# Reordering the first matrix products around the transposes at the start of a 2:4 sparse linear layer

## The chip, the cores and the metric

The kernel runs on one core of one Trainium2 chip. The metric is device time in microseconds (us) of one execution; lower is better. Before the change the median was 234.31 us over three executions (234.19 to 234.88).

Names: PE is TensorE, ACT is ScalarE, DVE is VectorE, SP is the engine that issues most loads, POOL is GpSimd. "Lnnn" in a profile is a line of the kernel's source.

## The reference, cut to what matters

```python
B, S, D = 16, 512, 1024
def reference(x, w, b):
    wg = w.reshape(G, M, D)                      # M = 4 rows of w to a group
    mag = jnp.abs(wg)
    order = jnp.argsort(mag, 1)
    thr = jnp.take_along_axis(mag, order[:, M - N:M - N + 1, :], 1)   # N = 2
    mask = (mag >= thr).astype(w.dtype)          # keeps the 2 largest of each 4
    wp = (wg * mask).reshape(D, D)
    return jnp.einsum("bsd,df->bsf", x, wp) + b
```

All types are bf16. The product has 8192 rows (64 tiles of 128), 1024 inputs and 1024 outputs.

## The kernel before

DVE has to prune the weights before the products can begin, so the kernel starts on what is ready first. Tiles 0 to 7 ("packed" tiles) are loaded plainly and transposed on PE; DVE prunes the weights in six pieces, and the products of these tiles with the first half of the inputs take the first four pieces (0 to 3) as DVE finishes them. The other 56 tiles come later through transposing loads. Each engine's program order in this start is a list of tokens:

- `T7a`: four PE transposes of x tile 7 into one of two PSUM banks. `C7a`: ACT copies that bank to SBUF.
- `M7.0x`: two products of tile 7 with the first half (x) of weight piece 0; `y` is the other half; `M7.2` is four products with piece 2.
- `S0b0`: ACT copies a finished PSUM bank of tile pair 0 (tiles 5 and 6) to a staging tile.
- `A0h1`: four products of the next group of tiles. `W1.0q`: two loads that spread pruned weights.

```python
    psum_t = ctx.enter_context(tc.tile_pool(name="psum_t", bufs=2, space=bass.MemoryType.PSUM))
    psum_o = ctx.enter_context(tc.tile_pool(name="psum_o", bufs=6, space=bass.MemoryType.PSUM))
    # ... loads, in program order on SP after the first weight loads:
    load_x(5, 7)
    load_x(0, 2)
    load_w(0, 256, 512)
    load_x(4, 5)
    load_x(2, 4)                 # x for tiles 2 and 3
    load_w(0, 512, 1024)
    # ...
    def transpose(t):            # T
        # ... bank from psum_t (two of them)
        for m in range(4):
            pe(nc.tensor.transpose(tp[:, m, :], xg[:, m, :], ident[:]))
    def copy_xt(t):              # C
        # ...
        act(nc.scalar.copy(xt[:].bitcast(fp32), xpk[t].bitcast(fp32)))
    def mm_piece(t, i, ms):      # M
        # ...
        for m in range(ms.start, ms.stop):
            # ...
            pe(nc.tensor.matmul(ps[:, c0 + d:c1 + d], lhsT=xpk[t][:, m, :], rhs=wp[:, g, m, c0:c1], ...))
    pairs = [(5, 6), (0, 1), (2, 3), (4, 7)]
    # ...
        "pe": (
            "F8 T7a T5a T6a T1a M5.0x M7.0x T0a M6.0x M6.0y M1.0x M7.0y M5.0y T3a M0.0y T4a M1.0y "
            "M0.0x T2a M3.0y M4.0x M3.0x M4.0y M2.0y M2.0x M4.1x M5.1x M0.1x ... "
            "... M3.3 M1.3 A0h0 A2h0 M7.3 A2h1 A1h0 A3h1 A0h1 A3h0 A1h1"
        ),
        "act": (
            "C7a C5a C6a C1a C0a C3a C4a S0b0 C2a S3b0 S1b0 S2b0 ... S1b3 S2b3 W1.0q S3b3 S0b3"
        ),
```

`T6a` waits for `C7a`, because there are two transpose banks; every later T waits in the same way for the C two transposes back.

Of the kernel before, what the change touches and what calls it, by code (L numbers as in the profile page):

```python
# [10 lines left out]
def kernel(  # L11
# [241 lines left out]
    def stage(q, n):  # L253
        if (q, n // 2) not in staged:
# [3 lines left out]

    order = {
        "pe": (  # L260
            "F8 T7a T5a T6a T1a M5.0x M7.0x T0a M6.0x M6.0y M1.0x M7.0y M5.0y T3a M0.0y T4a M1.0y "
            "M0.0x T2a M3.0y M4.0x M3.0x M4.0y M2.0y M2.0x M4.1x M5.1x M0.1x M7.1y M6.1y M2.1y "
            "M1.1y M3.1y M6.1x M4.1y M1.1x M3.1x M0.1y M7.1x M2.1x M5.1y M0.2 M3.2 M7.2 M1.2 M2.2 "
            "M4.2 M6.2 M0.3 M2.3 M5.3 M4.3 M5.2 M6.3 M3.3 M1.3 A0h0 A2h0 M7.3 A2h1 A1h0 A3h1 A0h1 "
            "A3h0 A1h1"
        ),
        "dve": (
            "abs0a hi0a abs0b lo0a hi0b lo0b t20 t10 thr0 mask0x mult0x mask0y mult0y abs1 lo1 hi1 "
# [2 lines left out]
            "thr5 mask5 mult5"  # L271
        ),
        "act": (
            "C7a C5a C6a C1a C0a C3a C4a S0b0 C2a S3b0 S1b0 S2b0 abs3 S3b1 S1b1 S0b1 S2b1 S2b2 S1b2 "
            "S3b2 S0b2 S1b3 S2b3 W1.0q S3b3 S0b3"
        ),
        "sp": (
# [213 lines left out]
```

## Time and profile before

| | before |
|---|---|
| median time | 234.31 us |
| span of the profiled execution | 232.5 us |
| PE busy | 227.5 us (98%) |
| granted clock | 1.00 |
| products after the packed start (L240) | 87% of the chain that ends last |

PE is the bound almost from start to end. The only room for a change of order is the time that PE stands still, and in the first 12 us that is well under 1 us. "Chain" is the sequence of work that ended last, followed backwards from the last instruction.

### The profile page before, as it was taken

To read this page: it belongs to the slowest core of one execution; us is meant where nothing else is said; L and a number is where in the kernel's file an instruction comes from. 1 tells how busy PE (TensorE), PEld (TensorE's weight loads), DVE (VectorE), ACT (ScalarE), POOL (GpSimd) and SP (SyncE) were. 2 spreads that over 40 slices of the span, in tenths; PEclk is the share of its full clock that TensorE was granted. 3 is DMA by queue.
4 is the path that set the end of the run, shared out by engine and by line. 5 is a ranking of instruction groups with operands and counts; after the bars stand their busy time and mean duration, and the time that the engine had idled before them with its cause. 6 is when DMAs were issued, how large, how long until landed. Compare 5 with 4: busy or idle time off the path is not lost.

```text
span 232.5 us, 2829 instructions
## 1 busy us (share of the span) xinstructions
PE 227.5 (98%) x1139; PEld 113.3 (49%) x1158; DVE 108.2 (47%) x185; ACT 13.7 (6%) x27; POOL 17.6 (8%) x15
## 2 busy tenths in 40 slices
PE   8999999999999999999999999999999999999995
PEld 5888444554444444444444444444444444444443
DVE  4999868864244244234334334324424424423434
ACT  2575100000000000000000000000000000000000
POOL 1000199700000000000000000000000000000000
PEclk9999999999999999999999999999999999999999
DMA  6999999996589521992249821696228931122122
GB/s 194 314 249 207 225 177 224 219 327 209 193 187 238 161 76 62 232 263 94 90 85 245 256 93 45 160 256 174 91 90 194 265 128 71 67 90 81 59 89 90
DMA packets 78268, 38.19 MB, mean 164 GB/s; under 512 B 63664, under 2 KB 70576, under 8 KB 78256
## 3 DMA queue, kind: packets, MB, share of 16 engines
q1 hardware_dynamic: 67600, 20.88, 44.0%
q10 hardware_dynamic: 10656, 17.14, 21.1%
q8 instruction: 9, 0.15, 0.3%
q14 instruction: 3, 0.02, 0.0%
HBM read 3.41 MB, written 16.78 MB: 87 GB/s over the span
## 4 chain that ended last, share of the span: by engine, by line
PE 94%; DMA 2%; SPq 1%; issue 1%; DVE 0%
PE ps L240 87%; PE ps L217 5%; DMA x<-in_x_dram 2%; PE tp L240 1%; SPq L100 1%; PE tp L191 0%; DVE o L400 0%
## 5 line engine op out<-in xcount | busy, mean ns | idle before, releaser
L240 PE MATMUL ps<-wp_nat,xb 128*128 128x512 bf16 (+2 forms) x832 | 178.9, 375 | 0.8
L240 PEld LDWEIGHTS <-xb 128*128 128x128 bf16 x848 | 82.4, 98 | 97.6
L400 DVE TENSOR_TENSOR o<-ps,bias_sb 128x512 bf16<-128x512 f32 (+1 forms) x112 | 71.5, 677 | 114.7 <-PE ps L240 110.3
L396 POOL TENSOR_TENSOR st<-st,bias_sb 128x1024 f32<-128x1024 f32 x8 | 16.7, 2127 | 0.0
L217 PE MATMUL ps<-wp,xt 128*128 128x256 bf16 x128 | 15.0, 273 | 0.0
L240 PE MATMUL ps<-wp_nat,xlow 128*128 128x512 bf16 x62 | 14.0, 379 | 0.1
L217 PEld LDWEIGHTS <-xt 128*128 128x128 bf16 x128 | 12.3, 98 | 1.6
L402 DVE TENSOR_TENSOR o<-ps,st 128x512 bf16<-128x512 f32 x16 | 11.1, 691 | 2.8 <-PE ps L240 2.1
L240 PE MATMUL ps<-wp_nat,xlead 128*128 128x512 bf16 x47 | 11.1, 379 | 0.1
L240 PEld LDWEIGHTS <-xlow 128*128 128x128 bf16 x64 | 7.2, 112 | 6.7
L240 PEld LDWEIGHTS <-xlead 128*128 128x128 bf16 x64 | 6.3, 98 | 7.1
L257 ACT COPY st<-ps 128x512 f32<-128x512 f32 x16 | 8.5, 594 | 6.1 <-PE ps L217 4.2
L156 DVE TENSOR_TENSOR wp<-w_sb,mag 128x512 bf16<-128x512 bf16 (+2 forms) x8 | 5.4, 690 | 0.2
L156 DVE TENSOR_TENSOR mag<-mag,hi 128x512 bf16<-128x512 bf16 (+2 forms) x8 | 5.4, 690 | 0.2
L135 PE MATMUL ps<-zeros 128*128 128x128 bf16 (+1 forms) x22 | 4.4, 400 | 1.0 <-DVE zeros L86 1.0
L240 PE MATMUL tp<-wp_nat,xlead 128*128 128x512 bf16 x16 | 4.1, 379 | 0.0
L191 PE MATMUL tp<-ident,x 128*128 128x128 bf16 x32 | 3.6, 260 | 0.3 <-DMA x<-in_x_dram 0.3
L135 PEld LDWEIGHTS <-zeros 128*128 128x128 bf16 x22 | 2.5, 147 | 2.6 <-issue 1.7
L166 DVE TENSOR_SCALAR mag<-w_sb 128x512 uint16<-128x512 uint16 (+2 forms) x6 | 2.7, 469 | 2.3 <-DMA w_sb<-in_w_dram 2.1
L191 PEld LDWEIGHTS <-x 128*128 128x128 bf16 x32 | 3.0, 130 | 0.8 <-DMA x<-in_x_dram 0.6
L156 DVE TENSOR_TENSOR hi<-mag 128x512 bf16<-128x512 bf16 (+2 forms) x7 | 3.2, 460 | 0.3 <-ACT mag L159 0.2
L196 ACT COPY xt<-tp 128x256 f32<-128x256 f32 x8 | 3.0, 375 | 4.3 <-PE tp L191 4.2
(16 smaller groups left out, 14.3 us busy)
## 6 DMA issues: line engine op xcount, KB each, us to landing
out_dram<-o ACTq DMA_DIRECT2D x59, 256.0 KB, 2.5
wp_nat<-wp SPq DMA_DIRECT2D x14, 128.0 KB, 3.4
w_sb<-in_w_dram SPq DMA_DIRECT2D x3, 512.0 KB, 7.0
out_dram<-o ACTq DMA_DIRECT2D x8, 128.0 KB, 1.7
x<-in_x_dram SPq DMA_DIRECT2D x3, 256.0 KB, 4.0
w_sb<-in_w_dram SPq DMA_DIRECT2D x1, 256.0 KB, 4.5
bias_sb<-in_b_dram SPq DMA_DIRECT2D x1, 256.0 KB, 7.0
wp_nat<-wp ACTq DMA_DIRECT2D x2, 128.0 KB, 3.5
```

The costliest lines, as they stand in the source:

```text
L100: return seq(eng, q.dma_start(out_, in_))
L135: pe(nc.tensor.matmul(warm_ps[:, :rep * P], lhsT=zeros[:], rhs=zeros[:, None, :].to_broadcast([P, rep, P]), start=True, stop=True))
L156: dve(nc.vector.tensor_tensor(out, a, b_, op=op))
L166: dve(nc.vector.tensor_single_scalar(self.mag[:, ms, :].bitcast(u16), self.w[:, ms, :].bitcast(u16), 0x7FFF, op=Alu.bitwise_and))
L191: pe(nc.tensor.transpose(tp[:, m, :], xg[:, m, :], ident[:]))
L196: act(nc.scalar.copy(xt[:].bitcast(fp32), xpk[t].bitcast(fp32)))
L217: pe(nc.tensor.matmul(ps[:, c0 + d:c1 + d], lhsT=xpk[t][:, m, :], rhs=wp[:, g, m, c0:c1], start=(new and m == ms.start), stop=(left[(q, n) ...
L240: pe(nc.tensor.matmul(ps, lhsT=xt[:, kt - koff, :], rhs=wp_nat[:, kt, c0:c1], start=(kt == first), stop=(kt == last)))
L257: act(nc.scalar.copy(st[:, n % 2, :, :].rearrange("p t c -> p (t c)"), ps_open.pop((q, n))[:]))
L396: pool(nc.gpsimd.tensor_tensor(st[:], st[:], bias[:, :, None, :].to_broadcast([P, 2, 2, CW]), op=Alu.add))
L400: dve(nc.vector.tensor_tensor(o[:, c0:c1], ps, bias_sb[:, c0:c1], op=Alu.add))
L402: dve(nc.vector.tensor_tensor(o[:, c0:c1].rearrange("p (n c) -> p n c", n=2), ps.rearrange("p (n c) -> p n c", n=2), add, op=Alu.add))
```

## The change

Its intent: keep PE from standing before the transpose of tile 3, whose x arrives late. The first products of tiles 7, 5 and 6 go ahead of the transposes of tiles 1 and 0; the transposes of tiles 3 and 2 go behind more of the first-piece products; ACT's copies follow the new order. Nothing is added or removed.

```diff
         "pe": (
-            "F8 T7a T5a T6a T1a M5.0x M7.0x T0a M6.0x M6.0y M1.0x M7.0y M5.0y T3a M0.0y T4a M1.0y "
-            "M0.0x T2a M3.0y M4.0x M3.0x M4.0y M2.0y M2.0x M4.1x M5.1x ...
+            "F8 T7a T5a T6a M7.0x M5.0x M6.0x T1a T0a M7.0y M5.0y M6.0y M1.0x M1.0y M0.0x T4a M0.0y "
+            "T3a T2a M4.0x M4.0y M3.0x M3.0y M2.0x M2.0y M4.1x M5.1x ...
         "act": (
-            "C7a C5a C6a C1a C0a C3a C4a S0b0 C2a S3b0 ...
+            "C7a C5a C6a C1a C0a C4a S0b0 C3a C2a S3b0 ...
```

## The prediction

> **What bounds the kernel now.** I read the page first, then the chain in order of time, then the waits of PE, then the first 30 us instruction by instruction. The page:
>
> ```profile
> PE 227.5 (98%) x1139; PEld 113.3 (49%) x1158; DVE 108.2 (47%) x185; ACT 13.7 (6%) x27; POOL 17.6 (8%) x15
> ...
> PE   8999999999999999999999999999999999999995
> ...
> PEclk9999999999999999999999999999999999999999
> ...
> PE 94%; DMA 2%; SPq 1%; issue 1%; DVE 0%
> ```
>
> TensorE (PE) is busy in every slice at the full granted clock, and 94% of the chain that ends last is PE. The change reorders PE and ScalarE (ACT) in the first 12 us only, so the question is how much PE stands still there. The chain in order of time says where it starts:
>
> ```profile
> 4.00 5.25 DMA x<-in_x_dram
> 9.25 0.05 issue
> 9.30 0.41 PE tp L191 x4
> 9.71 0.22 PE ps L217 x2
> 9.93 0.22 PE tp L191 x4
> 10.15 0.44 PE ps L217 x4
> 10.59 0.22 PE tp L191 x4
> 10.81 11.35 PE ps L217 x104
> ```
>
> The chain follows PE back without a break only to 9.30 us, and there to the load of x for tiles 2 and 3, issued at 4.00 and landed at 9.25. From 10.81 on it is 104 first-weight-half products back to back. The waits of PE agree; the first is the start of the fillers:
>
> ```profile
> PE ps L135 <- DVE zeros L86: 1.0, 1, 1.0
> PE tp L191 <- DMA x<-in_x_dram: 0.3, 1, 0.3
> ```
>
> The 0.3 understates it, as a matmul's reported end includes its modelled drain. Start to start: the last product before it (M5.0y) starts at 8.725, its slot is 0.109 us, so PE is free at 8.834 and T3 begins at 9.296: 0.46 us lost. The stretches show it (PE busy is the first figure after the comma; the four here are transposes and first products, more products, the wait, and the rest up to M4.1x):
>
> ```profile
> 5.23:7.08 1.85, 1.81 (x18) 1.65 (x17) 1.68 (x5) 0.88 (x3) 0.00 (x0) 1.00 1.06 310
> 7.08:8.84 1.76, 1.76 (x21) 1.51 (x18) 1.62 (x6) 0.95 (x3) 0.00 (x0) 1.00 0.87 282
> 8.84:9.30 0.46, 0.16 (x3) 0.01 (x1) 0.43 (x2) 0.00 (x0) 0.00 (x0) 1.00 0.86 274
> 9.30:11.96 2.66, 2.66 (x30) 2.47 (x31) 2.52 (x8) 1.75 (x5) 0.00 (x0) 1.00 1.05 352
> ```
>
> The other loss is a 0.24 us hole ahead of T6 (last T5 at 5.975 plus 0.107; first T6 at 6.325), which waits until C7 has emptied one of the two transpose banks.
>
> **What the Trainium skill says.** "TensorE: Matmul & The Clock Gate", section "Back-to-back issue gap", gives columns/1.2 ns cold and columns/2.4 + 2.5 ns warm. The trace agrees: transposes (128 columns) start every 0.107 us up to about 7.02 us and every 0.056 after it, products (256 columns) every 0.109. The same page, section "What's actually happening", calls the window that releases the clock free-running, so the 7.02 may move between executions; one trace can't show that. "Perfetto Trace Analysis", section "Tensor Engine Instruction (MATMUL, LD_WEIGHTS)", says a matmul's reported end is an estimate; hence I count start to start. "ScalarE: Activation LUTs", section "What ACT_TABLE_LOAD costs", says back-to-back activations overlap by about 93 ns; here, after a 0.372 us copy (C4 at 10.190), the next starts 0.268 later, an overlap of 0.104.
>
> **The change part by part.** Nothing is added or removed: PE has the same 2318 rows and ACT the same instructions. DVE keeps its order. So the sum is only of waits. I use these handover times from the trace: last transpose start + 0.219 (its duration, warm) + 0.037 to the copy's start; copy 0.372 + 0.05 to the PE instruction that needs it; 0.268 from one copy to the next on a busy ACT, 0.478 after a 0.59 us staging copy. Checked on the old order, this arithmetic puts M4.1x (first product of the second weight piece, where the two orders meet again) at 11.952; the trace has 11.960.
>
> *Part 1, M7.0x M5.0x M6.0x ahead of T1 T0.* To T6's end at 6.75 nothing differs. M7.0x needs C7 (done 6.27) and the first masked weights (6.226): no wait. It runs mostly cold and ends at 7.10; M5.0x ends at 7.32. M6.0x needs C6, done at about 7.37, and its handover at 7.42: a new wait of 0.10. M6.0x, then T1 7.64 to 7.87, T0 to 8.09. The old order had only T1 in the cold stretch; the new has M7.0x there, the same time. T1's and T0's banks have been emptied. So part 1 costs 0.10.
>
> *Part 2, more first products before the late transposes.* From 8.09: M7.0y M5.0y M6.0y M1.0x M1.0y M0.0x, six of 0.218 (C1 and C0 are done at 8.45 and 8.72, before they are needed), then T4 at 9.40 (its x landed at 7.45) and M0.0y at 9.62. T3 comes at 9.84, by which time its x has been there since 9.25: the 0.46 wait is gone, with 0.55 in hand. But T3 and T2 now stand side by side, and T2 takes the bank of T4: T4's last transpose starts at 9.565, C4 runs 9.82 to 10.20, T2 begins at 10.25 where PE was free at 10.06: a new wait of 0.19.
>
> *Part 3, ACT now C4 S0b0 C3 C2.* S0b0 (the staging copy of pair 0) starts 0.268 after C4, at 10.09. C3 must follow it by 0.478, at 10.57, although T3 was ready near 10.3. M4.0x M4.0y fill PE from 10.47 to 10.91; M3.0x needs C3 and starts near 11.00: a new wait of 0.09. C2 follows at 10.84 and holds up nothing. Then four products of 0.218, and M4.1x at 11.87.
>
> *Sum.* Removed 0.46 (0.44 in my arithmetic); added 0.10 + 0.19 + 0.09 = 0.38; rounding and the cold stretch leave a gain of about 0.08 us (11.952 to 11.868).
>
> *Does it reach the end?* PE then has to find later waits no closer than this. The tightest I found: A2h1 at 24.166 needs its four weight blocks, of which the last, landed at 23.51, is used at 24.814: 1.3 us in hand. A0h1 at 26.756 needs S0b3's bank, released at 26.32: about 0.4 in hand. A1h0 at 25.030 has its bank since 23.286. So a gain of 0.1 passes through the whole of the PE stream to the end: 234.31 - 0.08, about 234.2.
>
> **The rivals.**
>
> *The load wait is the whole story.* If the three new waits are absent (other handovers than I took), the gain is 0.46, giving 233.85. For it: the 0.46 is the only PE wait that the profile names after the fillers. Against it: T2 really does need C4, and the two are one M and one T apart.
>
> *The load lands later in most executions.* The old time moves one for one with that landing, the new one has 0.55 of slack. A load 0.3 later in the timed runs than in the profiled one makes the gain 0.38, giving about 233.9. One 0.6 earlier removes the old wait and makes the change lose about 0.38: 234.7. Landing took 5.25 us here, while the median of such loads is 4.0, so both are possible. DMA was 86% busy in that stretch, which speaks for the late side.
>
> *The clock opens at another time.* By the same arithmetic, were it warm from 6.0 the gain would be 0.33, since the old order just waits longer for its load; were it still cold until 8.0, the new order would be 0.28 behind, for it has no wait left to absorb slow matmuls. Against a large move: the timed runs spread over only 0.69 us (234.19 to 234.88).
>
> *Lost later.* ACT is nearer to the bound in 10 to 12 us, and a staging copy that comes later than a bank is needed would halt PE. S3b0 ends near 11.7 and M0.1x, which takes the bank that S3b0 frees in the new order, comes at about 12.3: not bound. This would make it 234.3.
>
> **Range and chances.** Centre 234.2. The gain lies between about -0.4 (an early load or a late clock) and +0.6 (a late load or an early clock); the medians of runs add some 0.3 of their own. That gives 233.6 to 234.8. A gain or a loss of 2% is 4.7 us. The PE idle time in all the first 12 us that this could touch is 0.7 us, and nothing in the diff alters the 220 us that follow, so 2% either way is out of reach except through a disturbed run: 0.01 faster, 0.985 within 2%, 0.005 slower.
>
> **What would show each step.** In the changed profile: the wait of a transpose for the load of x gone from PE's waits; T3 near 9.84; a gap of about 0.1 us before M6.0x at 7.4 and of about 0.2 before T2 at 10.25, released by ACT; C3 starting about 0.48 after S0b0, with M3.0x near 11.0; M4.1x at 11.87; from there the same spacing to the end, with the last product about 0.1 earlier. Part 2 is wrong if PE does not wait before T2; part 3 if C3 is not held by S0b0. The prediction as a whole would be wrong if PE shows new waits after 12 us, if the clock opens later than 7.0, or if the span shrinks by much more than 0.5 us.

## The result, and the profile after

The changed kernel takes 234.20 us (median of four, 234.01 to 234.62) beside 234.25 for the kernel before (median of four). The ratio is 0.9995 with a 95% interval of 0.9972 to 1.0018: the same. Ratios here are the mean time of one kernel's fast runs over the mean of the other's from the same rounds, so they are not quite the ratio of the quoted medians. A plain mean of all runs can differ a little (for no_waits_again, with one execution of 235.75, it gives 1.0001 beside 0.9992).

The page's PE line and its chain by engine have hardly moved:

```profile
PE 227.5 (98%) x1139; PEld 112.8 (49%) x1158; DVE 108.1 (47%) x185; ACT 13.3 (6%) x27; POOL 17.6 (8%) x15
...
PE 96%; DMA 2%; issue 1%; ACTq 0%; ACT 0%; DVE 0%
```

The chain after, in order of time (start, length, what), now reaches back through PE past 9.3 us:

```profile
5.52 0.63 PE tp L191 x4
6.17 0.38 ACT xt L196
6.60 0.38 PE tp L191 x4
6.98 0.44 PE ps L217 x4
7.44 0.39 PE ps L217 x2
7.84 0.45 PE tp L191 x8
8.28 1.31 PE ps L217 x12
9.59 0.22 PE tp L191 x4
9.82 0.22 PE ps L217 x2
10.04 0.22 PE tp L191 x4
10.28 0.38 PE tp L191 x4
10.66 11.47 PE ps L217 x104
```

The load of x for tiles 2 and 3 has left the chain. The waits of PE now name ACT's copies (engine, what waited, for whom: us in total, times, longest):

```profile
PEld L217 <- ACT xt L196: 0.5, 2, 0.3
...
PE tp L191 <- ACT xt L196: 0.2, 1, 0.2
```

PEld is the weight load ahead of a product. Its two waits are those of M6.0x (for C6) and M3.0x (for C3). The 0.2 of the second line is not new: it is T6 waiting for C7, ahead of all that the change touches. From start to start that hole was 0.24 us before and is 0.40 here, where the clock opened earlier and the transposes before T6 ran faster. T2's wait is too short for this view and shows only from start to start. As for the kernel before, I measure the PE loss from start to start, beyond the usual 0.109 us of a product or 0.056 of a transpose: 0.19 us before M6.0x (starts at 7.444), 0.18 before T2 (10.278) and 0.11 before M3.0x (11.044), together 0.48. (The 0.18 before T2 includes nothing of the load: it had landed at 8.54.) ACT's timeline shows why T2 and M3.0x wait:

```profile
9.85 0.37 ACT L196 COPY xt<-tp 128x256 f32<-128x256 f32 x1 [1.11 <-PE tp L191]
10.12 0.59 ACT L257 COPY st<-ps 128x512 f32<-128x512 f32 x1
10.60 0.67 ACT L196 COPY xt<-tp 128x256 f32<-128x256 f32 x2
```

These are C4, then the staging copy S0b0, then C3 and C2. C4 ends at 10.23, and T2 starts 0.05 later. C3 starts 0.48 us after S0b0, and M3.0x starts 0.05 after C3's end (10.99). M4.1x, where both orders meet again, starts at 11.929 instead of 11.960, and the last product at 229.592 instead of 229.623. The 0.03 us gained in front arrives whole at the end.

The two profiled executions were not alike, however. In the one after, x for tile 7 landed at 5.47 instead of 5.03 us, so PE began its transposes 0.29 us later; the start spacing shows the clock opening near 6.0 instead of 7.02; and the load of tiles 2 and 3 landed at 8.54 instead of 9.25. The experiments had to separate these from the change.

### The profile page after: what moved, and what is told of

Read it like the earlier page. It is cut to its first block, busy times and chain, and to the rows that moved or that the text cites. A ratio compares the mean times of both kernels' runs of the same rounds, so it can differ in the third digit from the quotient of the medians.

```text
span 232.5 us, 2829 instructions
## 1 busy us (share of the span) xinstructions
PE 227.5 (98%) x1139; PEld 112.8 (49%) x1158; DVE 108.1 (47%) x185; ACT 13.3 (6%) x27; POOL 17.6 (8%) x15
## 4 chain that ended last, share of the span: by engine, by line
PE 96%; DMA 2%; issue 1%; ACTq 0%; ACT 0%; DVE 0%
PE ps L240 87%; PE ps L217 6%; DMA x<-in_x_dram 2%; PE tp L240 1%; PE tp L191 1%; ACTq L100 0%; ACT xt L196 0%; DVE o L400 0%
## 5 line engine op out<-in xcount | busy, mean ns | idle before, releaser
L240 PE MATMUL ps<-wp_nat,xb 128*128 128x512 bf16 (+2 forms) x832 | 178.9, 375 | 0.8
L240 PEld LDWEIGHTS <-xb 128*128 128x128 bf16 x848 | 82.4, 98 | 97.5
L240 PE MATMUL ps<-wp_nat,xlow 128*128 128x512 bf16 x62 | 14.0, 379 | 0.1
L240 PE MATMUL ps<-wp_nat,xlead 128*128 128x512 bf16 x47 | 11.1, 379 | 0.1
L240 PEld LDWEIGHTS <-xlow 128*128 128x128 bf16 x64 | 7.2, 112 | 6.7
L240 PEld LDWEIGHTS <-xlead 128*128 128x128 bf16 x64 | 6.3, 98 | 7.1
L257 ACT COPY st<-ps 128x512 f32<-128x512 f32 x16 | 8.5, 598 | 6.2 <-PE ps L217 4.3
L240 PE MATMUL tp<-wp_nat,xlead 128*128 128x512 bf16 x16 | 4.1, 379 | 0.0
L191 PE MATMUL tp<-ident,x 128*128 128x128 bf16 x32 | 3.0, 231 | 0.3 <-ACT xt L196 0.2
L156 DVE TENSOR_TENSOR lo<-mag 128x512 bf16<-128x512 bf16 (+2 forms) x7 | 3.2, 456 | 0.0
```

The source lines that it names most:

```text
L156: dve(nc.vector.tensor_tensor(out, a, b_, op=op))
L240: pe(nc.tensor.matmul(ps, lhsT=xt[:, kt - koff, :], rhs=wp_nat[:, kt, c0:c1], start=(kt == first), stop=(kt == last)))
L257: act(nc.scalar.copy(st[:, n % 2, :, :].rearrange("p t c -> p (t c)"), ps_open.pop((q, n))[:]))
```

## The experiments

Twelve runs were made, of eleven kernels (no_waits_again is the kernel of no_waits once more). Eleven runs were correct; fewer_early was wrong, had one execution only, and is read from its profile alone. This is what the profiled execution of each shows, in us from the start of the span. "Landing" is that of x for tiles 2 and 3; "clock opens" is where the start spacing of PE halves or, where PE stood still at that moment, where the clock record kept in the trace has it (after_early has no such record, so a range stands there); "waits" are PE losses between T6 and M4.1x.

| kernel | landing | clock opens | waits | M4.1x | last product |
|---|---|---|---|---|---|
| before | 9.25 | 7.0 | T3 0.46 | 11.960 | 229.623 |
| after | 8.54 | 6.0 | M6.0x 0.19, T2 0.18, M3.0x 0.11 | 11.929 | 229.592 |
| before_late | 10.68 | 6.6 | T3 2.00 | 13.385 | 231.049 |
| after_late | 10.68 | 6.2 | M6.0x 0.19, T3 1.13 | 12.510 | 230.174 |
| before_early | 8.15 | 5.2 | none over 0.06 | 10.949 | 228.626 |
| after_early | 7.89 | 6.0 to 6.3 | M6.0x 0.19, T2 0.18, M3.0x 0.11 | 11.653 | 229.317 |
| part1 | 9.13 | 5.4 | M6.0x 0.19, M1.0x 0.19, T3 0.42 | 11.840 | 229.504 |
| part2 | 9.15 | under 5.0 | T1 0.06, T3 0.20, M3.0x 0.06 | 11.049 | 228.712 |
| no_waits | 8.97 | 6.9 | none | 11.394 | 229.127 |
| no_waits_early | 7.38 | 5.5 | none | 11.095 | 228.758 |
| no_waits_again | 9.00 | 9.9 | none | 13.392 | 231.055 |
| no_waits_free | 7.97 | 6.1 | none | 11.154 | 228.826 |
| no_waits_early_free | 8.14 | 6.1 | none | 11.154 | 228.818 |

The last two columns differ by 217.66 to 217.68 in every row but no_waits (217.73, see below). And the times. By the rule that asks for 2% every class here is "same"; what is compared below are differences of a few tenths of a per cent, with their intervals:

| kernel | median us | of | before, same rounds | ratio | 95% interval |
|---|---|---|---|---|---|
| before_late | 236.53 | 6 | 234.17 | 1.0107 | 1.0072 to 1.0142 |
| after_late | 234.90 | 6 | 234.17 | 1.0049 | 1.0016 to 1.0082 |
| before_early | 233.63 | 6 | 234.17 | 0.9981 | 0.9965 to 0.9997 |
| after_early | 233.99 | 6 | 234.17 | 0.9996 | 0.9980 to 1.0012 |
| part1 | 234.09 | 4 | 233.93 | 1.0005 | 0.9992 to 1.0019 |
| part2 | 234.18 | 4 | 233.93 | 1.0007 | 0.9987 to 1.0026 |
| no_waits | 233.95 | 5 | 233.93 | 1.0004 | 0.9991 to 1.0018 |
| no_waits_early | 233.41 | 5 | 233.93 | 0.9979 | 0.9965 to 0.9992 |
| no_waits_again | 233.78 | 7 | 234.08 | 0.9992 | 0.9977 to 1.0007 |
| no_waits_free | 233.62 | 6 | 234.08 | 0.9985 | 0.9971 to 1.0000 |
| no_waits_early_free | 233.49 | 5 | 234.08 | 0.9977 | 0.9963 to 0.9991 |

### The load late, in both orders

```diff
-    load_x(2, 4)
     load_w(0, 512, 1024)
+    load_x(2, 4)
```

> The kernel before with one edit: the load of x for tiles 2 and 3 is issued after the 512 KB weight load that used to follow it. Theory A (the old order waits for this load at T3, and its front moves one for one with the landing; M4.1x comes 2.7 us after the landing): landing near 10.7 to 11.2 us, PE waits for it for about 2 us, M4.1x at landing + 2.7, about 13.4 to 13.9 instead of 11.96, so the whole run 1.4 to 1.9 us longer than before (235.7 to 236.2). Rival B (the order of products, not this load, sets the front): M4.1x stays within 0.5 us of 11.96 and the time within 0.5 us of before.

> The changed kernel with the same late load. Theory A (T3 stands two products later, so it has some 0.5 us in hand, and with a late load the new waits of T2 and M3.0x vanish behind it; M4.1x comes 1.83 us after the landing): M4.1x at landing + 1.83, that is 0.88 us earlier than the old order with the same landing; time 0.9 us under that of before_late, about 0.5 to 1.0 us over before. Rival B (the new order is worth the same 0.03 to 0.1 us wherever the load lands): the two late kernels differ by no more than 0.1 us at M4.1x.

Both loads landed at 10.68 us, which makes this the cleanest pair. The chain of before_late:

```profile
4.59 6.08 DMA x<-in_x_dram
10.68 0.05 issue
10.72 0.41 PE tp L191 x4
11.14 0.22 PE ps L217 x2
11.36 0.22 PE tp L191 x4
11.58 0.44 PE ps L217 x4
12.02 0.22 PE tp L191 x4
12.24 11.35 PE ps L217 x104
```

The chain of after_late:

```profile
4.59 6.09 DMA x<-in_x_dram
10.68 0.05 issue
10.73 0.64 PE tp L191 x8
11.36 11.35 PE ps L217 x104
```

Between the same landing and the 104 products there are twelve transposes and six products in the old order, but only eight transposes in the new one. M4.1x came at landing + 2.71 and landing + 1.83; the theory had 2.7 and 1.83, and the difference of 0.875 us is at the last product too (231.049 against 230.174). Rival B of both runs, that this load does not set the front or that the change is worth the same wherever it lands, is out.

The median of before_late is longer than the trace explains. Three of its six executions had a mean granted clock of 0.993 and took 237.2, 237.9 and 237.8; the other three, at 1.000, took 235.3 to 235.9. One of six in after_late was like that (237.3). Without those four the means are 235.62 and 234.85, a difference of 0.77 beside the 0.875 of the traces.

### The load early, in both orders

```diff
-    load_x(4, 5)
     load_x(2, 4)
+    load_x(4, 5)
```

> The kernel before with the loads of x for tiles 2-3 and for tile 4 exchanged, so that the former lands earlier, near 8.0 to 8.5 us. Theory A: the wait of T3 for the load is gone (the old order is ready for it at 8.83), nothing takes its place, and M4.1x comes at about 11.5 instead of 11.96; time about 0.4 us under before. Rival C (waits for copies would take its place): M4.1x stays at 11.8 or later.

> The changed kernel with the same exchange. Theory A: the new order does not look at this load before 9.84, so an earlier landing gives nothing; its three waits for copies (before M6.0x, T2, M3.0x; 0.38 us in all) stay, and M4.1x is at 11.85 to 11.95 as without the exchange, some 0.4 us later than in before_early; the change is then a loss of about 0.4 us. Rival B: the change is never worse than the old order; M4.1x at or before that of before_early.

The waits of PE in before_early, from 4 us to 30 us, and then those in after_early:

```profile
PEld L191 <- issue: 0.3, 1, 0.3
PE tp L191 <- ACT xt L196: 0.2, 1, 0.2
```

```profile
PEld L217 <- ACT xt L196: 0.5, 2, 0.3
PEld L191 <- issue: 0.2, 1, 0.2
```

before_early keeps only the old hole ahead of T6, which waits for C7. after_early still has the three waits for copies, 0.48 us from start to start, unchanged from the profile after (the view lists M6.0x and M3.0x; T2's is again too short for it). So with an early load the change is a loss: M4.1x is 0.70 us later, of which 0.48 is the three waits; the other 0.22 is the later opening of the clock in that execution (T6, ahead of all that the change touches, already began 0.25 us later). The timed medians differ by 0.36 us. The expectation for before_early (11.5) was missed to the good side, because the clock opened at 5.2 and PE was fast from the first transpose. That for after_early (11.85 to 11.95) was missed too, with 11.653: it had reckoned with an opening at 7.0.

### Each part alone

part1 is the new front up to T0 with the rest as before; part2 is the old front with the new rest:

```diff
 part1
-T7a T5a T6a T1a M5.0x M7.0x T0a M6.0x M6.0y M1.0x M7.0y M5.0y T3a
+T7a T5a T6a M7.0x M5.0x M6.0x T1a T0a M6.0y M1.0x M7.0y M5.0y T3a
 part2
-T0a M6.0x M6.0y M1.0x M7.0y M5.0y T3a M0.0y T4a M1.0y M0.0x T2a M3.0y M4.0x M3.0x M4.0y M2.0y M2.0x
+T0a M6.0x M6.0y M7.0y M5.0y M1.0x M1.0y M0.0x T4a M0.0y T3a T2a M4.0x M4.0y M3.0x M3.0y M2.0x M2.0y
```

> Part 1 alone: M7.0x M5.0x M6.0x ahead of T1 T0, everything after as in the old order, the old order of ACT. Theory A: M6.0x waits for C6 (0.10 us if the clock opens at 7.0, 0.19 if earlier), which only uses up time that T3 would have waited for the load anyway: M4.1x at landing + 2.70 as in the old order where the load lands after 9.1, time as before within 0.1 us. Rival B (part 1 is what gains): M4.1x at least 0.1 us before landing + 2.70 with such a landing.

> Part 2 alone, with the new order of ACT: the old front with T1 ahead of the products, then T3 and T2 late and side by side. Theory A: no wait for the load, no wait of M6.0x, but T2 waits for C4 (0.18) and M3.0x for C3 (0.09 to 0.11); M4.1x at 11.63 to 11.76 wherever the load lands before 9.7, so 0.0 to 0.1 us ahead of the whole change. Rival B (part 1 and part 2 need each other): M4.1x later than the changed kernel's by over 0.1.

part1 behaves as theory A says: M6.0x waits 0.19 (and M1.0x 0.19 for C1, which I had not expected), T3 still waits 0.42 for the load, and M4.1x is at landing + 2.71, exactly as in the old order. Part 1 gains nothing where the load is the bound, and costs its wait where it is not.

In part2 the expected M4.1x of 11.63 to 11.76 was missed: it came at 11.05. The clock was open before the first transpose, which began at 4.98, so PE reached T3 ahead of the landing and waited 0.20; the wait for C4 lay inside that. The load was still on the path in this execution, but M4.1x at landing + 1.90, where part1 has 2.71, shows that part 2 is what shortens the way from the landing. Neither part moves the timed medians beyond their intervals.

### Without the three waits

```diff
-T6a M7.0x M5.0x M6.0x T1a T0a M7.0y M5.0y M6.0y M1.0x M1.0y M0.0x T4a M0.0y T3a T2a
+T6a M7.0x M5.0x T1a M6.0x T0a M7.0y M5.0y M6.0y M1.0x M0.0x T4a M0.0y T3a M1.0y T2a
-C7a C5a C6a C1a C0a C4a S0b0 C3a C2a S3b0
+C7a C5a C6a C1a C0a S0b0 C4a C3a C2a S3b0
```

no_waits_early has the exchanged loads of before_early as well.

> The changed kernel, its three new waits designed away: T1 stands ahead of M6.0x (covers C6), M1.0y stands between T3 and T2 (covers C4), and the staging copy S0b0 stands ahead of C4 (C3 is no longer behind it). The late T3 is kept. Theory A (the removed load wait was really worth 0.4 to 0.5 us, and the three copy waits gave it back): no PE wait between T6 and M4.1x but for at most 0.1 us at T1 and, if the load lands after 9.4, at T3; M4.1x 0.35 to 0.5 us earlier than the changed kernel would have it with the same opening of the clock (11.87 at 7.0, 11.62 at 6.2), so 11.1 to 11.5; time about 0.4 us under before, 233.7 to 233.9 where before is 234.2. Rival B (other waits grow in their place): M4.1x within 0.15 us of the changed kernel's, time as before.

> The same with the loads of tiles 2-3 and tile 4 exchanged. Theory A: with an early landing neither order waits for the load, so this equals the old order with the exchange: M4.1x 10.9 to 11.5 after the opening of the clock, time 233.5 to 233.8, no better than no_waits by more than 0.2 us. Rival: if the load still costs something in no_waits, this is 0.3 us or more better.

In the trace of no_waits all three waits are gone and nothing grew in their place before M4.1x, which comes at 11.394 with the clock opening at 6.9, against the 11.87 that the prediction's arithmetic gives the changed kernel with an opening at 7.0 (an estimate from the durations in the trace of before; 11.82 with the slip in Part 1 mended, see below). Its profiled execution took 233.78 us. The five timed executions do not show it: ratio 1.0004, so a gain over 0.2 us, some 0.09%, lies outside the interval. That half of the expectation failed. The profile held one more clue: 0.07 us were lost at A0h1 (26.264), which is why M4.1x to the last product is 217.73 here.

no_waits_early is faster than before, 0.9979, and 0.54 us under no_waits in the medians, so the rival of its expectation, that the load still costs something in no_waits, is what the times favour. But before_early, the old order with nothing but the two loads exchanged, has 0.9981: it too has neither the wait for the load nor the three for copies. The times do not show that the new order adds anything to the exchange.

### Is there a second bound behind the front?

A0h1 needs a PSUM bank that S3b3 empties. On ACT, S3b3 stands behind two DMA issues (W1.0q) that wait for DVE's fifth weight piece. no_waits_free takes S3b3 out from behind them; fewer_early takes 0.87 us of PE work out ahead of A0h1 (its result is wrong).

```diff
 no_waits_free
-"pe": ... M3.3 M1.3 A0h0 A2h0 M7.3 A2h1 ...
+"pe": ... M3.3 M1.3 M7.3 A0h0 A2h0 A2h1 ...
-"act": ... S1b3 S2b3 W1.0q S3b3 S0b3
+"act": ... S1b3 S2b3 S3b3 W1.0q S0b3
 fewer_early (on before_early), in mm_piece
         for m in range(ms.start, ms.stop):
             left[(q, n)] -= 1
+            if i == 3 and m == 1:
+                continue
```

> The kernel of no_waits once more, to stand beside the next two on the same chip. Its profiled run gained 0.53 us and its timed runs nothing. Theory D (a second bound behind the front: A0h1 waits for a bank that S3b3 empties, S3b3 stands on ACT behind two DMA issues that wait for DVE's fifth weight piece, and that moves with the landing of the weight loads, not with PE; in no_waits A0h1 already lost 0.07 us to it): 0.0 to 0.4 us under before. Rival E (chance in the timed runs): 0.4 us under before.

> no_waits with the tail's bank freed: M7.3 ahead of A0h0 on PE, and S3b3 ahead of the two DMA issues on ACT, so that A0h1 no longer waits on DVE's progress. Theory D: no PE wait at A0h1; the distance from M4.1x to the last product is 217.66 us in every run; 0.1 to 0.4 us faster than no_waits_again, 0.3 to 0.5 under before. Rival E: same time as no_waits_again within 0.1 us.

> The three together: no waits in the front, the loads of tiles 2-3 and 4 exchanged, the tail's bank freed. Theory D: 233.2 to 233.6, 0.5 to 0.7 us under before and the best of all; distance from M4.1x to the last product 217.66.

> Wrong on purpose: before_early with one in four products of the fourth weight piece left out, 8 of 0.109 us or 0.87 us of PE work, all ahead of A0h1. In before_early A0h1 just waited for S3b3 (0.016 us). Theory D: PE arrives at A0h1 up to 0.87 us earlier and waits; A0h1 still starts 0.05 us after the end of S3b3, near 25.6 to 26.3, so 0.7 us or more of the 0.87 is lost in waits and the last product is no more than 0.2 us earlier than in before_early, apart from the shift of S3b3 itself. Rival F (all PE time saved ahead of the tail shows in the end): distance from M4.1x to the last product 217.66 - 0.87 = 216.8.

The chain of fewer_early in 20 to 30 us shows the second bound bare:

```profile
22.75 1.22 DVE wp L156
23.97 0.61 DVE hi L156
24.59 0.05 ACTq L100
24.64 0.04 issue
24.68 0.89 ACTq L100
25.57 0.04 issue
25.61 0.59 ACT st L259
26.21 0.04 issue
26.25 1.02 PE ps L242 x4
```

(The two added source lines shift L257 to L259 and L240 to L242.) The path runs from DVE through ACT's DMA issues and S3b3 to A0h1 on PE. Its entry in the waits of PE:

```profile
PE ps L242 <- ACT st L259: 0.8, 1, 0.8
```

From start to start PE lost 0.94 us there and 0.39 more at 14.87, so the removed 0.87 us bought nothing: the last product starts at 229.113, even 0.49 after that of before_early, which is how much later S3b3 ended (26.199 against 25.711). From M4.1x to the last product it takes 218.12 us, where rival F has 216.8. Rival F is out: PE time saved ahead of A0h1 counts only down to that bank.

How much it matters in no_waits is less clear. In no_waits_free A0h1 has no wait and the best executions are a little better (233.37), but its median of 233.62 is only 0.16 under no_waits_again, inside the spread of either. The two timed expectations of theory D were met in number, but these runs cannot tell it from chance. The profiled execution of no_waits_again tells of something else. Its time is 235.75; the PE timeline:

```profile
4.26 1.17 PE L135 MATMUL ps<-zeros 128*128 128x128 bf16 x9
6.23 1.66 PE L191 MATMUL tp<-ident,x 128*128 128x128 bf16 x12 [0.80 <-DMA x<-in_x_dram]
```

The first x tile landed 1 us late, PE stood still after its fillers, and the clock opened only at 9.9 us, 3 us later than in no_waits. M4.1x came 2.0 us later than there. That the pause delayed the clock is not shown: it was seen in one execution.

Three versions have intervals clear of 1 on the fast side, and all three have the exchanged loads and none of the three waits for copies: no_waits_early at 233.41, no_waits_early_free at 233.49 and before_early at 233.63, with ratios 0.9979, 0.9977 and 0.9981, some 0.5 us faster than the kernel before. after_early, with the exchange and the three waits, is not among them (0.9996).

## Why the prediction was right

The time, 234.20 for a predicted 234.2, and the class are right. The mechanism, one wait for a load exchanged for three waits for copies, is right too. That the sizes cancelled so closely in the traces is partly luck, as the sum below shows. Taken by its own steps:

**The bound.** Right. The 217.66 us from M4.1x to the last product are the same before and after, so only the front counts.

**Part 1.** The wait before M6.0x was there, with 0.19 for a predicted 0.10. The size hung on the clock opening at 7.0: it opened at 6.0 in the profile after, so PE ran through M7.0x and M5.0x sooner, while C6 came no sooner relative to T6. The 0.10 was also misread: in the trace of before C6 runs from 6.946 to 7.318, so it is done at 7.32 and its handover is at 7.37, not 7.42. The same arithmetic with this mended gives a wait of 0.05 at an opening of 7.0, M4.1x at 11.82 and a gain of 0.13 (estimates).

**Part 2.** Right: T3 started at 9.871 for 9.84, without a wait, and T2's wait was 0.18 for 0.19. The late pair shows the removed wait by itself.

**Part 3.** Right: C3 started 0.48 after S0b0, and M3.0x waited 0.11 for 0.09.

**Sum.** M4.1x came at 11.929 for 11.87, because tile 7's x was late (0.29) while the clock opened early. The closeness is luck: two errors of opposite sign nearly cancelled. The gain was 0.03 us for 0.08, both far below what the times can resolve. Across the two profiled executions 0.46 us was exchanged for 0.48. (The prediction's count of 2318 PE rows is in no profile; the pages list 1158 weight loads and 1139 products in both, and both kernels have the same tokens.)

**The rivals.** "The load is the whole story" fell with the three waits. "The load lands at another time" is the one that lives: with a late landing the change gains 0.875 us in the traces, and with an early one it loses the 0.48 of its three waits. The profile after is itself a case of an early landing. The same arithmetic, with its late start, its clock and its landing at 8.54, puts the old order at 11.49 (an estimate), 0.4 ahead of the new. "The clock opens at another time" is real and larger than I gave it: openings from under 5.0 to 9.9 were seen in the profiles, and the one at 9.9 cost 2 us together with its late start. "Lost later" did not happen; the copy that ends near 11.7 is S3b0 (11.13 and 0.62 long), not S0b0, which ends at 10.72, and M0.1x started at 12.37 without a wait.

**Does it reach the end?** The conclusion held, the step was wrong. I took A0h1 to need S0b3, with 0.4 us in hand. It needs S3b3, which in the trace of before ends at 25.82; with the handover of 0.05 that leaves 0.88 us. before_early used all of this (A0h1 began 0.05 us after S3b3's end, with 0.016 lost), and fewer_early went past it.

**What stays open.** The timed gain of the three versions without waits but with the original loads is smaller than their traces suggest. The later bank can cap it and late first loads can hide it; both were seen in a profile, but their share over the executions was not measured, since only one execution of each kernel was read in detail.

## What to carry to other kernels

When an order is changed to hide one wait, work out for every moved instruction what it will now stand behind: here two transposes side by side met the depth of a two-bank pool, and a copy moved behind a longer copy. Here the removed wait, for a transfer, varied with the landing (8.54 to 9.25 us in the two profiles of the pair), while the waits for copies came out the same (0.19, 0.18, 0.11) in both profiles where no load hid them. So compare both orders with the transfer made early and late rather than in one profile each. And try the order of the loads first: exchanging two of them in the old order did as much here, within the intervals, as any reordering of PE. Before spending effort on the front, look for the next bound behind it, here a bank that an unrelated chain on DVE and ACT releases.

## What the Trainium skill lacked or had wrong

- "TensorE: Matmul & The Clock Gate", section "Part 4: PE-mode transpose", says that the full clock does not engage for transposes. Here it does: transposes start every 0.107 us before the clock opens and every 0.056 after it; in before_early they ran at 0.056 from the second one on. (They are issued with nc.tensor.transpose, and the profile calls them MATMUL. Whether they count as work that opens the clock, no run here tells.)
- The same page, section "Back-to-back issue gap", gives about 131 ns per product of 512 columns in a stream with weight loads. In all runs here they start every 0.216 us, each with its own weight load; its isolated formula of columns/2.4 + 2.5 ns fits (0.216).
- The same page, section "What's actually happening", has about 3.4 us of sustained work opening the clock. In one execution with a pause of about 1 us in the work (no_waits_again), it opened at 9.9 us, 8.9 us after the first filler. And of the two kernels that paused for 1.1 and 2.0 us after it had opened (after_late, before_late), 4 of 12 executions had a mean granted clock of 0.993 and took 2.0 to 2.5 us more than the others. These four were not profiled, so that the pause did it is not shown. No page has a figure for a single pause that is shorter than its window.
- No page that I read has the handovers on which such a front turns: 0.05 us from the end of an ACT copy to the PE instruction that waits for it, and 0.037 us from the end of a PE transpose, as the profile reports it, to the copy on an idle ACT.
